# Splitting the first weight load of a decode kernel by partitions: 16 and 112 in place of 128

## The chip, the cores and the metric

The kernel runs on one core of one Trainium2 chip. The metric is device time in microseconds (us). Where two kernels are compared, their runs alternate on the same chip. The profile names compute engines (here PE does the matmuls, DVE the vector work, ACT the scalar functions, and there is POOL), a sync engine (SP) that here issues the large loads, and 16 DMA engines that move the data. The loads are written to SBUF, to tiles of 128 partitions (rows). A load has landed when the last DMA engine has reported its part of it: the last of the 16 landings of wq is at 15.43 us, and the matmul that waits for them starts at 15.56.

## The reference

One decoding step of one transformer block, in bf16, batch 1, one new token:

```python
h  = x + attention(layernorm(x), k_cache, v_cache, wq, wo)   # 32 heads, 4096 cached positions, Dh = 128
h2 = h + geglu(layernorm(h), w_gate, w_up, w_down)           # 640 -> 1728 -> 640
# attention: q = layernorm(x) @ wq (640 x 4096); softmax(q k^T / sqrt(128)) v; then @ wo
```

The caches are 33.5 MB each, and wq is 640 x 4096, which is 5.24 MB. With one token there is little to compute for each byte, and all of it has to be read.

## The kernel before

All large loads are issued by the sync engine, in a fixed order: wq, then K and V of four heads at a time (4 MB each) into three slots in turn, then the weights that follow. The first ones:

```python
d_x = P.dma("scalar", x_row[:, :], A_x[0, :, :])
d_wq = [P.dma("sync", arena[:, :], A_wq[:, :].rearrange("(p c) n -> p (c n)", c=5))]
# ... K0, V0, K1 into slots 0, 1, 2; later loads wait until their slot has been used up:
landed[n] = [P.dma("sync", dst[:, i * w:(i + 1) * w], src[:, i * w:(i + 1) * w],
                   consumed[n - NSLOT] if n >= NSLOT else None) for i in range(parts)]
# ... (cut)
qd = T(q_proj, xl, *d_wq)      # the query projection waits for the layernorm of x and all of wq
# ... (cut)
P.emit({"sync": 2})            # the first two sync operations go ahead of the start barrier
```

Partition p of `arena` gets rows 5p to 5p+4 of wq, 40,960 contiguous bytes of HBM: one packet of a DMA engine. In the trace the load has 128 packets of that size, eight to each of 16 engines (joined where one starts as another ends, they form 16 chains of eight). q feeds the products with K (line 273, `prod`), and these free the slots for later loads.

The softmax here doesn't subtract the row's maximum and nothing guards it: scores larger than these inputs give would overflow.

## Time and profile before

| | before |
|---|---|
| time, median of 3 runs | 203.04 us (202.98 to 203.41) |
| span in the profile | 201.9 us |
| read from HBM | 84.23 MB at 417 GB/s |
| PE / DVE busy | 60% / 50% |
| last of 16 landings of wq | 15.43 us |

From the profile's page: the span; the share of DMA-engine time busy in 40 equal slices (in tenths) and the GB/s moved in each; the bytes; and the shares of the chain of waits that ended last.

```profile
span 201.9 us, 2505 instructions
...
DMA  9999999999999999999999999999999999999992
GB/s 357 414 404 467 428 415 416 422 448 458 430 415 422 415 445 448 435 424 416 422 435 441 438 435 424 416 428 441 448 419 435 399 425 437 419 408 435 412 409 113
...
HBM read 84.23 MB, written 0.00 MB: 417 GB/s over the span
...
DMA 64%; PE 16%; DVE 14%; issue 3%; SPq 2%
```

The DMA row is 9 nearly everywhere, and the chain is mostly DMA. The kernel is bound by its loads; the 415 to 450 GB/s of most slices is about what 16 engines give at the 27.05 GB/s measured for one below (433 GB/s).

From the timeline (start, length, engine, line, operation, and in brackets the idle time before and what ended it), the arrival of x, the query projection, and the first products with K:

```profile
1.29 0.50 ACTq L51 DMA_DIRECT2D x_row<-in_A_x_dram  x1
...
6.94 0.35 PE L233 MATMUL bank<-one_bf,x_row 1*128 1x1 bf16 x5 [6.94 <-DMA x_row<-in_A_x_dram]
...
15.56 3.88 PE L259 MATMUL bank<-arena,xlnB 128*32 128x512 bf16 x40 [7.21 <-DMA arena<-in_A_wq_dram]
...
25.14 4.49 DVE L273 TENSOR_TENSOR prod<-slot,qb 128x4096 bf16<-128x4096 bf16 x2 [4.95 <-DMA slot<-in_A_k_cache_dram]
```

The projection starts as soon as wq has landed, the products as soon as K0 has; x arrived long before. The packet records of the trace add what these views do not show. After a slow first wave (1.80 to 2.66 us) each wq packet takes 1.514 us, which is 40,960 B / 1.514 us = 27.05 GB/s for one engine. Thirteen of the engines begin by 1.32 us, the last at 2.05 us.

### The profile page before, as it was taken

How to read it: one execution, taken by the hardware profiler on the slowest of the kernel's cores; microseconds unless marked ns; L12 is line 12 of the kernel's file. 1: busy time of each engine (PE TensorE's matmuls, PEld its weight loads, DVE VectorE, ACT ScalarE, POOL GpSimd, SP SyncE). 2: the span in 40 equal slices, each digit the busy share in tenths (PEclk: the TensorE clock that was granted, in tenths of full speed). 3: DMA queues.
4: the chain of work that ended last, by engine and by line, in shares of the span. 5: the costliest groups of instructions: out<-in, count | busy, mean ns of one | idle time of the engine just before them, and what ended most of it. 6: DMA issues, size and time to landing. Idle time of an engine off the chain costs nothing.

```text
span 201.9 us, 2505 instructions
## 1 busy us (share of the span) xinstructions
PE 120.4 (60%) x1010; PEld 58.8 (29%) x1010; DVE 101.2 (50%) x106; ACT 61.1 (30%) x273; POOL 5.0 (2%) x14
## 2 busy tenths in 40 slices
PE   0107058537937668690968197727844887467395
PEld 0103023112312233150324032312331344267383
DVE  3201088517979847924791578277708760100221
ACT  2101004620563550670156125603640363100101
POOL 7200000000000000000000000000000000000000
PEclk9999657995799996997599859988995799955555
DMA  9999999999999999999999999999999999999992
GB/s 357 414 404 467 428 415 416 422 448 458 430 415 422 415 445 448 435 424 416 422 435 441 438 435 424 416 428 441 448 419 435 399 425 437 419 408 435 412 409 113
DMA packets 4335, 84.39 MB, mean 418 GB/s; under 512 B 482, under 2 KB 868, under 8 KB 1508
## 3 DMA queue, kind: packets, MB, share of 16 engines
q1 hardware_dynamic: 4322, 84.23, 97.8%
q8 instruction: 8, 0.13, 0.3%
q14 instruction: 3, 0.02, 0.0%
q10 hardware_dynamic: 2, 0.00, 0.0%
HBM read 84.23 MB, written 0.00 MB: 417 GB/s over the span
## 4 chain that ended last, share of the span: by engine, by line
DMA 64%; PE 16%; DVE 14%; issue 3%; SPq 2%
DMA slot<-in_A_k_cache_dram 42%; DVE prod L273 12%; DMA slot<-in_B_w_down_dram 11%; DMA slot<-in_A_v_cache_dram 11%; PE bank L281 11%; PE bank L310 3%; SPq L51 2%; DVE sc L288 2%; PE bank L319 1%; PE bank L447 0%; DVE out_row L460 0%; PE bank L330 0%; DVE RT L329 0%
## 5 line engine op out<-in xcount | busy, mean ns | idle before, releaser
L281 PE MATMUL bank<-prod,id_b 128*128 128x512 bf16 x256 | 75.4, 454 | 50.8 <-DVE prod L273 50.8
L273 DVE TENSOR_TENSOR prod<-slot,qb 128x4096 bf16<-128x4096 bf16 x32 | 72.4, 2285 | 31.1 <-DMA slot<-in_A_k_cache_dram 31.1
L292 ACT ACTIVATE p_bd<-sc,zero_t 32x32 bf16<-32x32 f32 x128 | 46.4, 362 | 86.3 <-DVE sc L288 85.1
L281 PEld LDWEIGHTS bank<-prod,id_b 128*128 128x128 bf16 x256 | 26.9, 113 | 99.4 <-DVE prod L273 63.1
L288 DVE TENSOR_REDUCE sc<-bank 128x32 f32<-128x512 f32 x32 | 22.0, 688 | 21.4 <-PE bank L281 21.4
L292 ACT ACTIVATION_READ_ACCUMULATOR p_bd<-sc,zero_t 32x1 f32 x128 | 23.5, 184 | 0.0
L310 PE MATMUL bank<-slot,p_bd 128*16 128x512 bf16 x256 | 17.3, 379 | 3.1 <-ACT p_bd L292 2.5
L310 PEld LDWEIGHTS bank<-slot,p_bd 128*16 128x16 bf16 x256 | 9.4, 89 | 7.3 <-ACT p_bd L292 3.0
L319 PE MATMUL bank<-po_sb,hs 128*16 128x128 f32 x64 | 8.4, 274 | 1.1 <-ACT po_sb L314 1.1
L348 PE MATMUL bank<-aP,arena 128*128 128x1 bf16 x160 | 6.7, 178 | 3.8 <-DMA arena<-in_A_wo_dram 3.8
L417 PE MATMUL bank<-hlnT,slot 128*128 128x1 bf16 (+1 forms) x140 | 6.7, 176 | 3.2 <-DMA slot<-in_B_w_gate_dram 3.2
L259 PE MATMUL bank<-arena,xlnB 128*32 128x512 bf16 x40 | 3.9, 565 | 7.2 <-DMA arena<-in_A_wq_dram 7.2
L348 PEld LDWEIGHTS bank<-aP,arena 128*128 128x128 bf16 x160 | 6.6, 131 | 3.9 <-DMA arena<-in_A_wo_dram 2.5
L314 ACT COPY po_sb<-bank 128x512 f32<-128x512 f32 x8 | 4.7, 585 | 9.6 <-PE bank L310 9.6
L417 PEld LDWEIGHTS bank<-hlnT,slot 128*128 128x128 bf16 (+1 forms) x140 | 6.3, 118 | 4.1 <-DVE hX L407 3.3
L319 PEld LDWEIGHTS bank<-po_sb,hs 128*16 128x16 f32 x64 | 5.5, 96 | 4.5 <-issue 2.1
L244 ACT ACTIVATE ln<-ln,eps_t 128x1 f32<-128x1 f32 x2 | 0.6, 294 | 20.3 <-DVE ln L242 20.3
L263 DVE CAST qb<-bank 128x512 bf16<-128x512 f32 x1 | 0.7, 692 | 9.6 <-PE bank L259 9.6
L404 DVE TENSOR_TENSOR hT<-xx,bank 128x5 f32<-128x5 f32 x1 | 0.2, 163 | 10.2 <-PE bank L348 10.2
L233 PE MATMUL bank<-one_bf,x_row 1*128 1x1 bf16 x5 | 0.4, 177 | 6.9 <-DMA x_row<-in_A_x_dram 6.9
L259 PEld LDWEIGHTS bank<-arena,xlnB 128*32 128x32 bf16 x40 | 1.6, 136 | 9.1 <-issue 9.0
L334 DVE TENSOR_SCALAR aT<-bank,rz 16x128 bf16<-16x128 f32 x2 | 0.7, 339 | 6.0 <-PE bank L319 6.0
(65 smaller groups left out, 26.3 us busy)
## 6 DMA issues: line engine op xcount, KB each, us to landing
slot<-in_A_k_cache_dram SPq DMA_DIRECT2D x8, 4096.0 KB, 21.4
slot<-in_A_v_cache_dram SPq DMA_DIRECT2D x7, 4096.0 KB, 17.5
arena<-in_A_wq_dram SPq DMA_DIRECT2D x1, 5120.0 KB, 15.4
slot<-in_A_v_cache_dram SPq DMA_DIRECT2D x2, 2048.0 KB, 20.0
arena<-in_A_wo_dram SPq DMA_DIRECT2D x1, 2560.0 KB, 27.3
slot<-in_B_w_gate_dram SPq DMA_DIRECT2D x1, 2160.0 KB, 16.3
arena<-in_A_wo_dram SPq DMA_DIRECT2D x1, 1920.0 KB, 31.5
slot<-in_B_w_up_dram SPq DMA_DIRECT2D x1, 1296.0 KB, 18.4
```

The costliest lines, as they stand in the source:

```text
L51: ev = self.op(eng, lambda e: e.dma_start(out, in_), *deps, dma=True)
L259: i = e.matmul(ps_q[hf][32 * j:32 * j + 32, :], xlnB[:, c, :], wq_j[:, c, j, 4 * hf:4 * hf + 4, :], start=(c == 0), stop=(c == 4))
L263: qa = V(lambda e: e.tensor_copy(qb[:, 0:4, :].rearrange("p g d -> p (g d)"), ps_q[0][:, :]), qd)
L273: m = V(lambda e: e.tensor_tensor(out=prod[:, s % 4, :, :], in0=kt[:, 32 * u:32 * u + 32, :], in1=qb[:, G, :].unsqueeze(1).to_broadcast([1 ...
L281: i = e.matmul(ps_f[s % 2][:, :], id_b[:, :], prod[:, s % 4, :, 16 * b:16 * b + 16], start=(b == 0), stop=(b == 7))
L288: reds[s] = V(lambda e: e.reduce_sum(sc[:, s % 4, :], ps_f[s % 2][:, :].rearrange("p (g d) -> p g d", d=16), axis=AX.X), folds[s], exps.ge ...
L292: x = A(lambda e, j=j: e.activation(p_bd[32 * j:32 * j + 32, G % 2, 32 * (s % 4):32 * (s % 4) + 32, j], sc[32 * j:32 * j + 32, s % 4, :], ...
L310: i = e.matmul(po[a:a + 16, :], p_bd[:, G % 2, 4 * b:4 * b + 4, :].rearrange("p g j -> p (g j)"), vt[:, 4 * b:4 * b + 4, :], start=(b < 4) ...
L314: evs[G] = A(lambda e: e.copy(po_sb[:, G % 2, :], po[:, :]), pvs[G], hds.get(G - 2))
L319: i = e.matmul(ps_a[0:16, 128 * (G // 4):128 * (G // 4) + 128], hs[:, r, 12 - 4 * g:28 - 4 * g], po_sb[:, G % 2, 128 * r:128 * r + 128], s ...
L348: r = e.matmul(ps_p[:, c:c + 1], wo_sb[:, t, i, c::5], aP[:, t, i:i + 1], start=(t == 0 and c == 0 and i == 0), stop=(t == 1 and i == 15), ...
L417: i = e.matmul(ps[0:128 if m < 13 else 64, m:m + 1], ws, hlnT[:, c:c + 1], start=(c == 0 and m == 0), stop=(c == 4), skip_group_check=True)
```

## The change

The intent is that a first load of one row for each engine gets all sixteen engines going sooner than a load of eight rows each does (the last began at 2.05 us). The rest follows in a second load. The count of early sync operations goes from 2 to 3, so that wq and K0 still go ahead of the start barrier.

```diff
-    d_wq = [P.dma("sync", arena[:, :], A_wq[:, :].rearrange("(p c) n -> p (c n)", c=5))]
+    wq_v = A_wq[:, :].rearrange("(p c) n -> p (c n)", c=5)
+    d_wq = [P.dma("sync", arena[lo:hi, :], wq_v[lo:hi, :]) for lo, hi in ((0, 16), (16, 128))]
@@
-    P.emit({"sync": 2})
+    P.emit({"sync": 3})
```

## The prediction

> **What bounds the kernel now.** The loads. The page shows 84.23 MB read at 417 GB/s over a 201.9 us span, and a DMA row of 9s in 39 of 40 slices; PE is busy 60%, DVE 50%. The chain of waits is 64% DMA. A load's rows are dealt out over 16 DMA engines, eight each; in the packet records one 40,960-byte row of wq takes an engine 1.514 us (27.05 GB/s). The sync engine's timeline shows 22 us between a mid-kernel load's issue and its landing (149.2 to 171.4), so two loads are always queued. DMA time lost or won at the start should reach the end almost whole.
>
> **What the change does.** Same bytes, same compute; the order of instructions is the same but for one more sync DMA, and the three first issues (wq twice, K0) stay ahead of the start barrier.
>
> - *Added:* one issue, 0.33 to 0.42 us in the timeline; the barrier, passed at about 1.26 us, moves to about 1.7. Off the path: the query projection idles 7.2 us for wq until 15.5.
> - *Intended gain:* first packets start at 1.01 to 1.32 us on 13 engines, but at 1.64, 1.71 and 2.05 on three; the last engine's part of wq lands at 15.43 us, the next at 14.66. If every engine first gets one row, the latest may start up to 0.7 us sooner. Instruction fetches later make other engines nearly as late (the last load's landings spread over 197.65 to 199.63 us, the two latest 0.2 apart), so I expect 0.1 to 0.4 us at the end.
> - *Feared cost:* [...] Nothing in the kernel before shows it: its large loads all span 128 partitions. [...] Then the 112 rows come in sevens[...]. [...]
>
> **Prediction.** [...] 207 to 214 us (chance two in three); if not, 202.5 to 203.5. Predicted 208.5 us, range 202.5 to 214.5. Chances: faster by over 2% 0.02, within 2% 0.33, slower by over 2% 0.65.
>
> **What would show it.** Right: the first 16 packets take about 6 us instead of 2.2, GB/s in the first slice falls to near 110; many of the 112 rows' packets take 2 to 4.5 us; the first wq matmul moves from 15.5 us to 19 to 24, K0's first product from 25.1 to 30 or later, and everything after by a constant; later 32-kB packets still take 1.21 us. Wrong: first packets near 2 us, later ones 1.51, wq landing at 14.8 to 15.6, total within 0.5 us.
>
> **What would make it wrong.** [...] an interleaved deal[...] (far slower); or unseen slack.

The feared cost had been put at +4.5 us for the first load and at up to 6 us more for the 112 rows, 10.6 us in total for the slowest engine; with the 203.1 us of the kernel before that comes to 213.7. The 207 to 214 us are for the case that this cost is there. That the 112 rows come in sevens the trace after shows: its 128 packets of wq form 16 chains of eight, one packet of the first load and seven of the second.

## More of the kernel before

The start, in five-microsecond windows. After the window and its length come busy time and instruction count of each engine, the granted PE clock, the DMA busy share, and GB/s. A packet counts where it begins, so a window is uncertain by some packets.

```profile
core 0: us, PE busy (x) PEld busy (x) DVE busy (x) ACT busy (x) POOL busy (x), PEclk, DMA share, GB/s
0.00:5.00 5.00, 0.00 (x0) 0.00 (x0) 1.61 (x8) 1.28 (x1) 3.87 (x12) 1.00 0.94 344
5.00:10.00 5.00, 0.95 (x7) 0.78 (x7) 1.45 (x6) 0.59 (x2) 1.16 (x3) 1.00 1.00 434
10.00:15.00 5.00, 0.00 (x0) 0.00 (x0) 0.00 (x0) 0.00 (x0) 0.00 (x0) 1.00 0.87 375
15.00:20.00 5.00, 3.88 (x40) 1.57 (x40) 0.50 (x1) 0.50 (x1) 0.00 (x0) 1.00 1.05 452
20.00:25.00 5.00, 0.00 (x0) 0.00 (x0) 0.19 (x1) 0.08 (x1) 0.00 (x0) 0.71 1.08 465
25.00:30.00 5.00, 2.50 (x6) 0.89 (x7) 4.49 (x2) 0.00 (x0) 0.00 (x0) 0.50 1.02 439
30.00:35.00 5.00, 4.44 (x16) 1.65 (x15) 3.87 (x4) 1.99 (x10) 0.00 (x0) 0.76 0.97 419
```

## The result, and the profile after

| | before | after |
|---|---|---|
| median of 6 runs | 203.12 us | 215.63 us |
| span in the profile | 201.9 us | 214.1 us |
| first wq matmul | 15.56 us | 27.82 us (+12.26) |
| first product with K0 | 25.14 us | 37.43 us (+12.29) |
| last landing of the last weights | 199.63 us | 211.80 us (+12.17) |

The kernel is slower: ratio 1.0594 (95% interval 1.0561 to 1.0627). A ratio is the mean time of one kernel's fast runs over the mean of the other's fast runs of the same rounds, so it is not quite the ratio of the medians in the table.

The page after, the same lines:

```profile
span 214.1 us, 2506 instructions
...
DMA  9989899999999999999999999999999999999993
GB/s 122 245 245 245 214 435 441 416 465 392 462 416 418 459 404 447 419 423 455 410 453 416 423 444 416 455 410 435 441 410 450 416 410 432 430 415 426 408 415 129
...
HBM read 84.23 MB, written 0.00 MB: 394 GB/s over the span
...
DMA 58%; DVE 19%; PE 14%; issue 4%; another core or an unknown queue 2%; SPq 2%
```

The first five slices carry 122 to 245 GB/s; from the sixth on, the row looks like that of before. The busy row still says 8 and 9 there. A packet counts as busy time for as long as it lasts, and here the packets last 2 to 5 us in place of 1.51 (table below), so the busy share does not show this loss (1.00 in the first window), and GB/s does (131).

The windows after:

```profile
core 0: us, PE busy (x) PEld busy (x) DVE busy (x) ACT busy (x) POOL busy (x), PEclk, DMA share, GB/s
0.00:5.00 5.00, 0.00 (x0) 0.00 (x0) 1.61 (x8) 1.28 (x1) 3.41 (x11) 1.00 1.00 131
5.00:10.00 5.00, 0.00 (x0) 0.00 (x0) 0.29 (x1) 0.00 (x0) 1.61 (x4) 1.00 1.11 229
10.00:15.00 5.00, 0.00 (x0) 0.00 (x0) 0.00 (x0) 0.00 (x0) 0.00 (x0) 1.00 1.01 279
15.00:20.00 5.00, 0.95 (x7) 0.78 (x7) 1.15 (x5) 0.59 (x2) 0.00 (x0) 1.00 0.92 221
20.00:25.00 5.00, 0.00 (x0) 0.00 (x0) 0.00 (x0) 0.00 (x0) 0.00 (x0) 1.00 0.87 208
25.00:30.00 5.00, 2.18 (x24) 1.00 (x28) 0.00 (x0) 0.00 (x0) 0.00 (x0) 1.00 0.98 387
30.00:35.00 5.00, 2.28 (x24) 0.65 (x16) 0.69 (x1) 0.58 (x1) 0.00 (x0) 1.00 0.97 419
```

The timeline after:

```profile
1.75 0.51 ACTq L51 DMA_DIRECT2D x_row<-in_A_x_dram  x1
...
15.16 0.35 PE L234 MATMUL bank<-one_bf,x_row 1*128 1x1 bf16 x5 [15.16 <-DMA x_row<-in_A_x_dram]
...
27.82 4.46 PE L260 MATMUL bank<-arena,xlnB 128*32 128x512 bf16 x40 [11.26 <-DMA arena<-in_A_wq_dram]
...
37.43 4.49 DVE L274 TENSOR_TENSOR prod<-slot,qb 128x4096 bf16<-128x4096 bf16 x2 [4.41 <-DMA slot<-in_A_k_cache_dram]
```

The wq matmul is 12.26 us late, K0's product 12.29 us, and the span 12.2 us longer. The delay arises in the wq load and is carried unchanged to the end, 185 us later. x also arrives late (used at 15.15 us for 6.93): its one packet starts at 12.21 us instead of 5.00; why, the trace does not show. That costs nothing, as wq is later still.

The packet records do not name the engine. Taken sixteen at a time in order of their start, as waves of one packet for each engine, they took:

```
wave           1      2      3      4      5      6      7      8      median us of 16 packets
before        2.26   1.51   1.51   1.51   1.51   1.51   1.51   1.51
after         4.98   3.35   2.86   2.16   2.38   2.73   2.90   2.66
              (first load)  (the 112 rows, seven for each engine)
```

The first wave is over at 7.18 us instead of 4.50 (+2.7). The next seven, to the end of the last packet, take 19.6 us (7.18 to 26.80) instead of 10.6 (4.50 to 15.08), so +9.0. The issue that was added costs 0.45 us of the sync engine, which has nothing else to do then.

### The profile page after: what moved, and what is told of

Its sections match the earlier page's. It is cut to its first block, busy times and chain, and to the rows that moved or that the text cites. A ratio compares the mean times of both kernels' runs of the same rounds, so it can differ in the third digit from the quotient of the medians.

```text
span 214.1 us, 2506 instructions
## 1 busy us (share of the span) xinstructions
PE 119.6 (56%) x1010; PEld 58.3 (27%) x1010; DVE 101.1 (47%) x106; ACT 61.1 (29%) x273; POOL 5.0 (2%) x14
## 4 chain that ended last, share of the span: by engine, by line
DMA 58%; DVE 19%; PE 14%; issue 4%; another core or an unknown queue 2%; SPq 2%
DMA slot<-in_A_k_cache_dram 37%; DVE prod L274 15%; DMA slot<-in_B_w_down_dram 10%; DMA slot<-in_A_v_cache_dram 10%; PE bank L282 9%; DVE sc L289 3%; PE bank L311 3%; SPq L51 2%; PE bank L320 1%; PE bank L448 0%; DVE out_row L461 0%; PE bank L331 0%; DVE RT L330 0%
## 5 line engine op out<-in xcount | busy, mean ns | idle before, releaser
L282 PE MATMUL bank<-prod,id_b 128*128 128x512 bf16 x256 | 72.5, 440 | 51.5 <-DVE prod L274 51.5
L282 PEld LDWEIGHTS bank<-prod,id_b 128*128 128x128 bf16 x256 | 26.0, 110 | 98.8 <-DVE prod L274 65.1
L289 DVE TENSOR_REDUCE sc<-bank 128x32 f32<-128x512 f32 x32 | 22.0, 687 | 19.9 <-PE bank L282 19.9
L311 PE MATMUL bank<-slot,p_bd 128*16 128x512 bf16 x256 | 18.8, 409 | 3.3 <-ACT p_bd L293 2.5
L260 PE MATMUL bank<-arena,xlnB 128*32 128x512 bf16 x40 | 4.5, 631 | 11.3 <-DMA arena<-in_A_wq_dram 11.3
L265 ACT CAST qb<-bank 128x512 bf16<-128x512 f32 x1 | 0.6, 585 | 14.7 <-PE bank L260 14.7
## 6 DMA issues: line engine op xcount, KB each, us to landing
slot<-in_A_v_cache_dram SPq DMA_DIRECT2D x2, 2048.0 KB, 19.9
```

Source lines behind the costliest of these rows:

```text
L260: i = e.matmul(ps_q[hf][32 * j:32 * j + 32, :], xlnB[:, c, :], wq_j[:, c, j, 4 * hf:4 * hf + 4, :], start=(c == 0), stop=(c == 4))
L282: i = e.matmul(ps_f[s % 2][:, :], id_b[:, :], prod[:, s % 4, :, 16 * b:16 * b + 16], start=(b == 0), stop=(b == 7))
L289: reds[s] = V(lambda e: e.reduce_sum(sc[:, s % 4, :], ps_f[s % 2][:, :].rearrange("p (g d) -> p g d", d=16), axis=AX.X), folds[s], exps.ge ...
L311: i = e.matmul(po[a:a + 16, :], p_bd[:, G % 2, 4 * b:4 * b + 4, :].rearrange("p g j -> p (g j)"), vt[:, 4 * b:4 * b + 4, :], start=(b < 4) ...
```

## The experiments

The theory: the time of a load depends on which partitions of SBUF it writes at once, because some of them slow one another; in the load of all 128 a packet takes 1.51 us. The rivals: any second load, or any load narrower than 128 partitions, has a fixed cost; or the rows that are read in HBM matter.

All runs gave the same verdict on the output as the kernel before; what that is worth is told at the crossed runs.

### The same split by columns (`e1_columns`)

```diff
-    d_wq = [P.dma("sync", arena[lo:hi, :], wq_v[lo:hi, :]) for lo, hi in ((0, 16), (16, 128))]
+    d_wq = [P.dma("sync", arena[:, lo:hi], wq_v[:, lo:hi]) for lo, hi in ((0, 2560), (2560, 20480))]
```

> The wq load is split by columns in place of rows: a first load of 128 partitions x 2560 columns, with exactly the 655 kB of the change's first load, then 128 x 17920. The number of loads, of issues and of early issues is that of the changed kernel; only the rows that each load reaches differ. [...] no cost, 202.7 to 203.4 us, the first packets (5120 B) short, wq landing at 14.8 to 15.6 us. Rival (the second load, its issue or its completion costs the time): near 215 us as in the changed kernel.

Measured: 203.2 us in the median against 203.2 us, ratio 0.9999 (0.9969 to 1.0028). Two loads with the bytes and early issues of the changed kernel cost nothing that can be measured (the interval is about 0.6 us to either side), so neither the second load nor its issue is the cause of 12.5 us. From its timeline:

```profile
15.13 3.97 PE L260 MATMUL bank<-arena,xlnB 128*32 128x512 bf16 x40 [6.09 <-DMA arena<-in_A_wq_dram]
...
24.73 4.49 DVE L274 TENSOR_TENSOR prod<-slot,qb 128x4096 bf16<-128x4096 bf16 x2 [4.89 <-DMA slot<-in_A_k_cache_dram]
```

This form does give the intended head start: wq and K0 are about 0.4 us earlier than before (15.13 for 15.56, 24.73 for 25.14), and the last engine's part of wq lands at 14.99 us instead of 15.43. The end does not measurably move. In the landings and packet records the lead is lost between 44 and 55 us: K1's last landing is still earlier (44.13 for 44.56 us), K2's is not (55.02 for 54.80). A 16,384 B instruction fetch takes a DMA engine for about 1 us there (at 44.55 us here; at 45.53 us before, where it took 1.04). In both traces some other engine then lands last, and a load has landed only when its last engine has. That is read from one trace of each (the profiled run here was the slowest of its six, 204.15 us); no run took the fetch away.

### Eight loads of 16 partitions: neighbours, or every eighth (`e2_neigh16`, `e3_stride8`)

```diff
-    d_wq = [P.dma("sync", arena[lo:hi, :], wq_v[lo:hi, :]) for lo, hi in ((0, 16), (16, 128))]
+    d_wq = [P.dma("sync", arena[16 * i:16 * i + 16, :], wq_v[16 * i:16 * i + 16, :]) for i in range(8)]   # e2_neigh16
+    d_wq = [P.dma("sync", arena[i::8, :], wq_v[i::8, :]) for i in range(8)]                               # e3_stride8
```

In both, `emit` has `{"sync": 9}`, so that the eight loads and K0 stay ahead of the barrier.

> wq in eight loads of 16 neighbouring partitions each. [...] in all 48.4 us instead of 12.1: about +36 us, 239 us in total, packets of 40,960 B taking about 6 us each. Rival (each load that is not 128 partitions wide costs some fixed time, 2.7 us as the first load of the changed kernel did): +20 us or so, the same as for the strided loads.

> wq in eight loads of 16 partitions each, every eighth partition (0, 8, ... 120, then 1, 9, ...). Same number and size of loads as with 16 neighbours[...]. [...] packets of about 3.03 us, 24.2 us for wq instead of 12.1, so about +12 us, 215 us in total. Rival (a fixed cost for each load, or for any load of 16 partitions): the same time as with 16 neighbours.

Measured: 236.81 us with neighbours, 216.91 us with every eighth, against 203.2 us. The loads are as many and as large in both; only which partitions go together differs, and the extra time is 33.6 against 13.7 us (ratios 1.1644, 1.1606 to 1.1683, and 1.0665, 1.0625 to 1.0706). A fixed cost for each narrow load is refuted. After the first wave the packets take 5.77 us and 3.17 us in the median (1.51 in the kernel before). From the timelines, the wq matmul, first with neighbours, then with every eighth:

```profile
48.75 4.46 PE L260 MATMUL bank<-arena,xlnB 128*32 128x512 bf16 x40 [27.36 <-DMA arena<-in_A_wq_dram]
```

```profile
28.56 3.79 PE L260 MATMUL bank<-arena,xlnB 128*32 128x512 bf16 x40 [12.22 <-DMA arena<-in_A_wq_dram]
```

### Two halves (`e4_halves`)

```diff
-    for lo, hi in ((0, 16), (16, 128))]
+    for lo, hi in ((0, 64), (64, 128))]
```

> wq in two loads of 64 partitions (0 to 63, 64 to 127), four rows to an engine. [...] every packet takes about 3.03 us, wq 24.2 us instead of 12.1: +12 us, 215 us. Rival (fixed cost for each narrow load): +3 to +6 us, packets back at 1.51 us after each load's first.

Measured: 216.5 us, ratio 1.0645 (1.0610 to 1.0679); after the first wave, packets of 3.20 us in both loads to the end. So each of these halves is written at about half the rate of all 128 (1.51 us a packet), and with four rows for each engine the packets take as long as with one row of every eighth partition (3.17 us).

### Crossed: where it is written against where it is read (`e5_neigh_src8`, `e6_stride8_srcn`)

```diff
+    d_wq = [P.dma("sync", arena[16 * i:16 * i + 16, :], wq_v[i::8, :]) for i in range(8)]   # e5_neigh_src8
+    d_wq = [P.dma("sync", arena[i::8, :], wq_v[16 * i:16 * i + 16, :]) for i in range(8)]   # e6_stride8_srcn
```

> Wrong result on purpose. Eight loads of 16 rows as before, written to 16 neighbouring partitions each, but read from every eighth row of wq in HBM. If the cost lies in the partitions that are written[...]: packets of 5.8 us and about 237 us, as with 16 neighbours on both sides (236.8). If it lies in the rows that are read: packets of 3.2 us and about 217 us, as with every eighth row on both sides (216.9).

> Wrong result on purpose. The other half of the cross: written to every eighth partition, read from 16 neighbouring rows of wq. [...] 3.2 us packets, about 217 us. Rows read: 5.8 us packets, about 237 us.

(In the second text, the 3.2 us are for a cost that lies in the partitions written.)

Measured, one run each, so of unknown state: 236.11 us written to neighbours (packets 5.64 us), 216.45 us written to every eighth (3.19 us). The time follows the partitions that are written; the rows that are read make under 1 us of difference (236.81 and 216.91 us uncrossed). The cost is on the SBUF side. Both kernels multiply x with permuted rows of wq, and the comparison with the reference still passed them, so it is not fine enough to see an error in q.

### The 112 rows as seven loads (`e7_sevens`)

What had no explanation yet was the second load. At seven packets of 1.514 us an engine it would take 10.6 us, and the forecast's term added up to 6; the load took 19.6 us. Either each engine gets other rows than seven consecutive ones, or the cost of rows that slow one another is larger than was reckoned.

```diff
-    d_wq = [P.dma("sync", arena[lo:hi, :], wq_v[lo:hi, :]) for lo, hi in ((0, 16), (16, 128))]
+    d_wq = [P.dma("sync", arena[0:16, :], wq_v[0:16, :])] + \
+           [P.dma("sync", arena[16 + i::7, :], wq_v[16 + i::7, :]) for i in range(7)]
```

> The load of 112 rows is replaced by seven loads of 16 rows, rows 16+j, 23+j, ... 121+j for j = 0 to 6: what a deal of seven consecutive rows to each engine would do in its j-th step. If the 112-row load deals consecutive sevens, this must repeat it: about 215.6 us, packets of 2 to 3 us on all engines. [...]

(The alternative: 207 to 213 us if the rows are dealt in another way.)

Measured: 215.32 us (after: 215.63), ratio to before 1.0582 (1.0519 to 1.0646). The waves repeat those of the changed kernel, one by one:

```
wave           1      2      3      4      5      6      7      8      median us of 16 packets
after         4.98   3.35   2.86   2.16   2.38   2.73   2.90   2.66
e7_sevens     4.88   3.46   2.88   2.16   2.32   2.69   2.90   2.60
```

So the 112-row load behaves as if each engine had seven consecutive rows, and what is left to explain is why sixteen rows seven apart take 2.2 to 3.5 us and not 1.51. The wq matmul starts 0.12 us from that of the changed kernel:

```profile
27.70 3.68 PE L260 MATMUL bank<-arena,xlnB 128*32 128x512 bf16 x40 [12.99 <-DMA arena<-in_A_wq_dram]
```

### Patterns by themselves (`p1_probe`, `p2_steady`, `p3_pairs`)

These kernels put loads of 32 kB rows of K into places that are still free, wait for each pattern, and then run the unchanged kernel. Their totals (290.45, 355.18 and 358.30 us, one run each, of unknown state) mean nothing; the packets of each pattern do.

```diff
+    # p1_probe: one load of each pattern, each waiting for the one before
+    for rows in (slice(0, 128), slice(0, 128), slice(11, 117, 7), slice(0, 128, 8), slice(0, 46, 3),
+                 slice(0, 16), slice(0, 106, 7), slice(16, 128)):
+        last = P.dma("sync", slots[2][rows, 0:128 * DH], k1[rows, :], last)
+    # ... then the seven loads slots[2][16 + i:122 + i:7] together
+    # p2_steady, p3_pairs: each pattern five times in a row, into three slots, arena and prod
+    for rows in (...):                     # the patterns of the table below
+        now = []
+        for to in places:
+            now.append(P.dma("sync", to[rows, :], k1[rows, :], *last)); last = []
+        last = now
```

> Loads of 32 kB rows into the third slot, one after the other, each waited for, ahead of the unchanged kernel: 128 rows (warm-up), 128 rows, [...] the 112 rows 16 to 127, and the seven loads of every seventh row together. [...] 1.21 for the 128 rows[...], 2.5 for every eighth, up to 3.7 for every third, 4.6 for 16 neighbours. [...] The 112 rows: 2.2 a packet on average, and about 15 us; the seven loads the same if sevens are dealt consecutively. [...] Total about 284 us.

(Rows 11, 18, ... 116 were expected at the 1.21 us of the 128 rows, or, by the rival, as slow as the other narrow loads; rows 0, 7, ... with four packets of 2.4 us and twelve of 1.21, or all at about 2.2.)

Measured in `p1_probe`: the single packets were blurred by their slow start, and the numbers expected for them were not met. They took 1.42 to 1.98 us for rows 11, 18, ... 116, 1.82 to 2.65 for every eighth, 2.43 to 3.77 for every third, 3.09 to 4.15 for 16 neighbours. The order is the expected one, and rows 11, 18, ... were fastest though the load is as narrow as the others, against the rival. The 112 rows took 16.4 us and the seven loads together 15.9 us, which again agrees with consecutive sevens. Rows 0, 7, ... gave six packets of up to 1.70 us and ten of 2.03 to 2.66, so more than four slow ones, and not all alike; the next run looks at that in steady state.

> Steady state of single patterns ahead of the unchanged kernel: each pattern is loaded five times over into five places (three slots, arena, prod), 32 kB rows, so every engine has five packets in line (40 for the 128-row pattern), and the next pattern waits for all five. [...] What is open: in the changed kernel all sixteen engines were slowed in the 112-row load[...]. Theory A[...]: rows 3, 10, ...[...]: two engines at 2.3 to 2.4 us, fourteen at 1.21; rows 0, 7, ...[...]: four slow, twelve fast; rows 0, 5, ... 35[...]: two slow, six fast. Theory B[...]: rows 3, 10, ...: nine slow, seven at 1.21; rows 0, 7, ...: ten slow, six at 1.21; rows 0, 5, ... 35: all eight slow. Both: rows 11, 18, ...[...] and rows 0, 4, ... 28[...]: all 1.21; rows 0 and 1[...]: 2.3 to 2.4 both; every third row: 2.4 to 3.6.

> As the run before, other patterns, to tell why rows 0, 7, ... held up all sixteen engines at 2.49 us while rows 3, 10, ... held up only the two[...]. Theory C[...]: rows 5, 12, ..., rows 9, 16, ... and rows 14, 21, ...[...] have all sixteen packets at 2.4 to 2.5 us; rows 4, 11, ... and rows 7, 14, ...[...] have two engines at 2.4 and fourteen at 1.21; rows 0, 3, ... 21[...] all eight at 2.4 to 2.5; rows 0, 6, ... 42[...] two at 2.4, six at 1.21. Rival (rows 0, 7, ... are a special case[...]): the three patterns[...] have four engines at 2.4 and twelve at 1.21.

Measured in `p2_steady` and `p3_pairs`, the steady packets of each engine. The engines were told apart by joining each packet to the one that starts where it ends. Which rows an engine carried, the records do not say. The slow first packets and single longer ones (up to 2.2 us, spread over the engines) are left out.

```
rows             engines  us of a 32 kB packet
11, 18 .. 116      16     1.21 on all
0, 4 .. 28          8     1.21 on all
3, 10 .. 108       16     2.41 on two, 1.21 on fourteen
4, 11 .. 109       16     2.41 on two, 1.21 on fourteen
7, 14 .. 112       16     2.41 on two, 1.21 on fourteen
0, 5 .. 35          8     2.41 on two, 1.21 on six
0, 6 .. 42          8     2.56 on two, 1.21 on six
0, 7 .. 105        16     2.49 on all sixteen
5, 12 .. 110       16     2.51 on all sixteen
9, 16 .. 114       16     2.49 on all sixteen
14, 21 .. 119      16     2.51 on all sixteen
0, 3 .. 21          8     2.4-2.5 on four, 2.1-2.2 on four
0, 3 .. 45         16     4.26 on all sixteen
0, 1                2     2.57 on both
```

For rows 3, 10, ... and for rows 0, 5, ... 35 theory A of `p2_steady` holds: two engines take twice as long (2.41 us), nobody else notices (1.21). For rows 0, 7, ... neither A nor B holds: all sixteen engines of the load slow down to 2.49 us, where A had twelve and B had six at 1.21. Theory C, formed from that, was met by six of the seven patterns of `p3_pairs` and nearly by the seventh: of the eight engines of rows 0, 3, ... 21, four took 2.4 to 2.5 us as expected and four were a little faster, at about 2.15 us, which is still far from 1.21. Every third row of 0 to 45 is slowest (4.26 us). Rows 0 and 1, by themselves, take 2.57 us each, over twice the 1.21. Why some sets have two slow engines and others have all slow is not settled; these runs show only that they do. Nor were these patterns crossed as wq was: each reads the same rows of K that it writes in SBUF, so that the side of this effect is taken over from the crossed runs, not shown here.

Windows within single patterns show the same as a rate; the columns are as above. In `p2_steady`, first 128 rows, then rows 0, 7, ...:

```profile
10.00:50.00 40.00, 0.00 (x0) 0.00 (x0) 0.00 (x0) 0.00 (x0) 0.00 (x0) 1.00 1.01 435
80.00:90.00 10.00, 0.00 (x0) 0.00 (x0) 0.00 (x0) 0.00 (x0) 0.00 (x0) 1.00 0.91 190
```

In `p3_pairs`, rows 5, 12, ..., then 9, 16, ..., then 14, 21, ...:

```profile
56.00:65.00 9.00, 0.00 (x0) 0.00 (x0) 0.00 (x0) 0.00 (x0) 0.00 (x0) 1.00 0.89 186
85.00:94.00 9.00, 0.00 (x0) 0.00 (x0) 0.00 (x0) 0.00 (x0) 0.00 (x0) 1.00 0.85 178
144.00:153.00 9.00, 0.00 (x0) 0.00 (x0) 0.00 (x0) 0.00 (x0) 0.00 (x0) 1.00 0.91 189
```

A window of this length counts the slow first packets and cuts waves at its edges; at the steady 2.50 us a packet the rate is 16 x 32,768 B / 2.50 us = 210 GB/s. Rows 0, 7, ... are thus loaded at half the 435 GB/s of the 128 rows, hardly faster than every eighth row of wq in `e3_stride8` (16 x 40,960 B / 3.17 us = 207 GB/s).

## Why the prediction was right or wrong

- **What bounds the kernel, and that a delay at the start is carried to the end: right.** The matmul on wq moved by 12.26 us, the span by 12.2.
- **The added issue is off the path: right.** The column split has it too and costs nothing.
- **The intended gain: not there.** In its trace the row split did not start the last engine sooner at all (latest first packet 2.25 us, before 2.05). The column split gained 0.4 us at the start and nothing in the medians (203.2 us for both); a gain of the 0.1 to 0.4 us forecast is too small for these runs to exclude.
- **The feared cost: it was there, its second term was mis-sized.** That a load of fewer partitions can be written more slowly was borne out (5.77 us a packet in `e2_neigh16`, 3.17 in `e3_stride8`, 3.20 in `e4_halves`, 1.51 before). For the first load the prediction had +4.5 us. Measured: +2.7. In part this is because the first wave takes 2.26 us instead of 1.51 in any case, and 16 neighbours took 5.77 us a packet in `e2_neigh16` and not the 6 or so expected; the rest, first packets of 4.98 us where steady ones of that pattern take 5.77, was not explained. For the 112 rows it had up to 6 us more, 10.6 in total for the worst engine. Measured: +9.0 us for that load, 11.7 us to the last packet and 12.26 to the last landing. The deal in consecutive sevens was as assumed (`e7_sevens`, 215.32 us for 215.63). What failed is the reckoning of what such rows cost, which let part of the engines go on at full rate: in four of the eight sets of sixteen rows seven apart in the probes, all sixteen engines slow down to about 2.5 us. An estimate from `p1_probe`: its 112 rows of 32,768 B took 16.4 us and its seven loads 15.9 us; in proportion to the 40,960 B of a wq row that is 20.5 and 19.9 us; measured 19.6. How the single steps add up to that is not shown: none of the seven was probed in steady state, and the changed kernel does not show them cleanly (wave 5 starts, at 14.54 us, before wave 4 is over, at 15.93).
- **The range and the number: wrong.** 208.5 us is near the mean, weighted by the chances, of its two outcomes (about 203 and 207 to 214), and the range ended at 214.5, below the 215.63 measured. Its two terms together, +10.6 us, would have given 213.7; that this is only 2 us short is luck, as the first term was too large and the second too small. Of its risks a dearer interleaved deal is left in the text, and a lower cost (about +4 us) is among those cut; that all sixteen engines of a load could slow down at once was in neither.
- **The signs named under "Right" were met but for one:** first packets of 4.98 us in the median (about 6 named), 122 GB/s in the first slice (near 110), packets of 1.9 to 3.8 us in the 112 rows (2 to 4.5), later 32 kB packets still at 1.218 us (1.214 before), and a constant shift. The wq matmul, at 27.82 us, lay beyond the 19 to 24 named.

No version beat both kernels: the column split ties with the kernel before.

## What to carry to other kernels

Split a load by columns rather than by partitions, so that each piece still spans all 128 partitions; here that made the difference between 203.2 and 215.6 us. Before shrinking the partition range of a load on a DMA-bound path, measure the packets of the very set of partitions that is written at once: sixteen rows of 32 kB took 1.21 us each for rows 11, 18, ... 116, but 2.49 for rows 0, 7, ... 105 and 4.26 for rows 0, 3, ... 45. Read GB/s, not the DMA busy share: the busy row stayed at 8 or 9 tenths while the rate was halved.
